# An attention and snake-MLP kernel: alpha loaded as 16 rows and transposed on TensorE, and the first w_in load cut to 256 columns

## The chip, the cores and the metric

The kernel runs on one core of a Trainium2 chip. The metric is the device time of one execution in microseconds, given as the median of several runs; beside it there is one execution taken by the hardware profiler. Engines are named as in the profile: PE is TensorE (PEld its weight loads), DVE is VectorE, ACT is ScalarE, POOL is GpSimd, SP is SyncE. A "q" behind an engine's name is its sequencer or its queue.

## The reference

Two stages. The first is chunked attention: 4 batches, 8 heads, 768 positions, head size 64. Each chunk of 32 queries sees 8 memory keys and up to 56 context keys (16 to the left, 32 of its own, 8 to the right).

```python
for c in range(nc):                       # 24 chunks of 32
    k_full = concat([mem_k, k[:, :, l_start:r_end]], axis=2)
    v_full = concat([mem_v, v[:, :, l_start:r_end]], axis=2)
    a = softmax(q_c @ k_full.T / sqrt(64))
    out[:, :, c_start:c_end] = a @ v_full
```

The second stage takes its output as x, with 3072 tokens of 512 numbers, and computes an MLP with 2048 inner columns:

```python
h = x @ w_in                              # 512 -> 2048
s = sin(alpha * h)                        # alpha: 2048 numbers, one per inner column
g = h + s * s / (alpha + 1e-09)
return g @ w_out                          # 2048 -> 512
```

## The kernel before, in words

Work is split by batch. For each batch of 768 tokens there is an attention part that fills `xT` (the transposed x) and an MLP part: 16 steps `ft` of 128 inner columns each (`l1`: 8 matmuls of 128x384 at line 400, a sine on ACT, a square on ACT, DVE or POOL, and a fused multiply-add on DVE into `gT`), and then the second matrix product (`l2`), whose pieces are mixed into the next batch's work by a `Stream`.

Batch 0 has nothing to overlap with but its own loads, and its attention part is written out by hand. `ORDER` is a string of pieces; `first_burst` walks through it, and every engine gets its instructions in that order. The pieces are: `k n` and `q n` transpose a pair of heads of k or q on PE (line 246, after some dummy matmuls on zeros at line 162, `spin`), and copy them out (k on DVE at lines 251 and 257, q on ACT, but `q 1` on DVE, line 264). `memk` transposes the memory keys on PE (line 363), copies them on DVE (line 367) and spreads them into `kTi` (line 149). `memv` converts the memory values and spreads them into `vw` (DVE, lines 142 and 143). `s n` are scores (PE, line 271), `e n` exponentials (ACT, line 287), `v n` the product with v (PE at line 302, DVE at 306 and 307), `x n` the transpose into `xT` (PE at line 323, a copy at line 326), `z n` dummy matmuls. The order starts:

```python
"k 0,q 0,memk 0,memv 0,k 1,s 0,e 0,z 1,s 1,e 1,q 1,k 2,s 2,e 2,s 3,v 0,q 2,..."
```

Loads go through two queues. SP's holds, in this order, mem_k in four parts (line 179), mem_v (line 180), and alpha (line 195), and later the stores of the output. POOL's holds the loads that change the type from float32 to bfloat16, in the order of the program: k pair 0, q pair 0, k 1, q 1 (line 107), the first quarter of v in four parts (line 139), k 2, q 2, k 3, q 3, the other three quarters of v in twelve parts, w_in in four parts (line 203), k and q of batch 1 (line 120), and w_out in two parts (line 209). [...] There are eight semaphores for these loads in turn, so each of them waits until the load eight places ahead of it has landed.

alpha is wanted as `alpha_sb`, 128 partitions by 16 columns, so that each `ft` has its 128 numbers down the partitions. The load before reads the vector of 2048 numbers in that transposed order: each element of four bytes goes to its own place. `inv_alpha` is computed from it on DVE (line 496) after the first burst, and the sines read `alpha_sb` as their scale (lines 409 and 412).

In PSUM there are two pools: `big` with three buffers of two banks, and `smp` with two buffers of one bank (tag `sm`), which the dummy matmuls, the q transposes, `memk` and others take in turn.

Of the kernel before, what the change touches and what calls it, by code (L numbers as in the profile page):

```python
# [9 lines left out]
P = 128  # L10
# [7 lines left out]
BF = mybir.dt.bfloat16  # L18
F32 = mybir.dt.float32
# [30 lines left out]
def kernel(  # L50
# [12 lines left out]
    nc = tc.nc  # L63
# [5 lines left out]
    HP = H // 2  # L69
    FT = d_ff // P  # L70
# [4 lines left out]
    consts = ctx.enter_context(tc.tile_pool(name="consts", bufs=1))  # L75
# [6 lines left out]
    smp = ctx.enter_context(tc.tile_pool(name="smp", bufs=2, space=bass.MemoryType.PSUM))  # L82
# [4 lines left out]
    ident = consts.tile([P, P], BF, name="ident")  # L87
# [8 lines left out]
    memkT = consts.tile([P, HP, 32], BF, name="memkT")  # L96
# [2 lines left out]
    memv_f = consts.tile([P, B, H, D], F32, name="memv_f")  # L99
    w_in_sb = consts.tile([P, KT, d_ff], BF, name="w_in_sb")  # L100
    w_out_sb = consts.tile([P, FT, d_model], BF, name="w_out_sb")
    alpha_sb = consts.tile([P, FT], F32, name="alpha_sb")
    inv_alpha = consts.tile([P, FT], F32, name="inv_alpha")

    def load_qk_pair(b, hp, kb, qb):
        for src, dst in ((k, kb), (q, qb)):
            nc.gpsimd.dma_start(
                dst[:, 2 * hp:2 * hp + 2].rearrange("p h r d -> p h (r d)"),
                src[b, 2 * hp:2 * hp + 2].rearrange("h (p r) d -> p h (r d)", p=P),
            )  # L110
# [15 lines left out]
    def load_v(b, n0, n1):  # L126


        vw = vws[b % 2].rearrange("p h j c -> p (h j) c")
        vf = v[b].rearrange("h s d -> (h s) d")  # L130
        vf = vf.rearrange("(n p) d -> p n d", p=QW)
        parts = (
            (vw[16:64, n0:n1, 0:D], vf[0:48, n0:n1]),
            (vw[72:120, n0:n1, 0:D], vf[48:96, n0:n1]),
            (vw[0:16, n0 + 1:n1, 0:D], vf[80:96, n0:n1 - 1]),
            (vw[120:128, n0:n1 - 1, 0:D], vf[0:8, n0 + 1:n1]),
        )
        for dst, src in parts:
            nc.gpsimd.dma_start(dst, src)  # L139

    def put_memv(b):
        (nc.vector.tensor_copy if b == 0 else nc.scalar.copy)(memv_st[64:72, b], memv_f[64:72, b])
        nc.vector.tensor_copy(
            vws[b % 2][64:72, :, :, 0:D],
            memv_st[64:72, b].unsqueeze(2).to_broadcast([NM, H, NJ, D]),
        )

    def put_memk(b):
        nc.vector.tensor_copy(
            kTi[:, :, 24:KW].rearrange("p g (j c) -> p g j c", c=104)[:, :, :, 40:40 + NM],  # L150
            memkT[:, :, NM * b:NM * b + NM].unsqueeze(2).to_broadcast([P, HP, NJ, NM]),
        )
# [4 lines left out]
    def spin(n, z=None):  # L157

        if z is None:
            z = smp.tile([P, 512], F32, name="z", tag="sm")  # L160
        for _ in range(n):
            nc.tensor.matmul(z[:], zeros[:, 0:P], zeros[:])  # L162
# [12 lines left out]
    load_v(0, 0, 16)  # L175
    for hp in range(2, HP):
        load_qk_pair(0, hp, *kq)
    for b in range(B):
        nc.sync.dma_start(memk_f[NM * b:NM * b + NM], mem_k[b].rearrange("h n d -> n h d"))
    nc.sync.dma_start(memv_f[64:72].rearrange("n b h d -> n (b h) d"),  # L180
                      mem_v.rearrange("b h n d -> n (b h) d"))
    for c, (a, e) in enumerate(((0, 16), (16, 56), (64, 120), (120, P), (32, 96), (64, 72))):
# [4 lines left out]
    nc.vector.tensor_add(rows[:, 3:4], rows[:, 2:3], rows[:, 3:4])  # L187
    nc.vector.tensor_scalar(
        out=biasm[:], in0=rows[:, 0:5], scalar1=1.0, scalar2=-NEG, op0=ALU.subtract, op1=ALU.mult)
    nc.scalar.copy(memk_bf[:], memk_f[:])  # L190
    load_v(0, 16, 32)
    load_v(0, 32, 48)
    load_v(0, 48, 64)
    with nc.allow_non_contiguous_dma(reason="alpha transpose load"):
        nc.sync.dma_start(alpha_sb[:], moe_alpha.rearrange("(ft p) -> p ft", p=P))

    nc.vector.memset(kTi[:, :, 0:16], 0.0)
    nc.vector.memset(kTi[:, :, 848:856], 0.0)
# [3 lines left out]
    def load_w_in(c0, c1):  # L202
        nc.gpsimd.dma_start(
            w_in_sb[:, :, c0:c1],
            moe_w_in[:, c0:c1].rearrange("(kt p) f -> p kt f", p=P),
        )
# [42 lines left out]
    def t_k(kb, hp):  # L249
        t = turn(kb, hp, hp < 2)  # L250
        nc.vector.tensor_copy(
            kTi[:, hp, 72:72 + 7 * 104].rearrange("p (s c) -> p s c", c=104)[:, :, 0:96]
            .rearrange("p s (a r) -> p s a r", r=6),
            t[:, :, 8:120].rearrange("p r (s a) -> p s a r", a=16),
        )
        for t0, c0 in ((0, 16), (120, 800)):
            nc.vector.tensor_copy(
                kTi[:, hp, c0:c0 + 48].rearrange("p (a r) -> p a r", r=6),
                t[:, :, t0:t0 + 8].rearrange("p r a -> p a r"),
            )  # L260

    def t_q(qb, hp, copy=nc.scalar.copy):
        t = turn(qb, hp)
        copy(qT[:, hp, :].rearrange("p (a r) -> p a r", r=6), t[:, :, :].rearrange("p r a -> p a r"))

    def qk(cells):

        sc = big.tile([P, 2, 512], F32, name="sc", tag="big")
        for c, (hp, j) in enumerate(cells):
            for e in range(2):  # L270
                nc.tensor.matmul(  # L271
                    sc[:, e, QW * c:QW * c + QW],
                    kTi[64 * e:64 * e + 64, hp, 104 * j:104 * j + P],
                    qT[64 * e:64 * e + 64, hp, QW * j:QW * j + QW],
                )
        return sc

    def exps(cells, sc):
        pt = pts[state["n"] % NPT]
        state["n"] += 1  # L280
        for m in range(3):
            cols = [((1 if j == 0 else 0), 4, (2 if j == NJ - 1 else 3))[m] for _, j in cells]
            c0 = 0
            for c1 in range(1, 5):
                if c1 < 4 and cols[c1] == cols[c0]:
                    continue
                nc.scalar.activation(  # L287
                    pt[:, 0:H * QW].rearrange("p (g e c) -> p e g c", g=4, e=2)[:, :, c0:c1, 32 * m:32 * m + 32],
                    sc[:, :, 0:4 * QW].rearrange("p g (e c) -> p g e c", e=4)[:, :, c0:c1, 32 * m:32 * m + 32],
                    ACTF.Exp, bias=biasm[:, cols[c0]:cols[c0] + 1], scale=0.125,  # L290
                )
                c0 = c1
        return pt
# [20 lines left out]
    def xt(dst, x_blk, ot, copy=nc.vector.tensor_copy, warm=0):  # L314
        if ot is None:
            z = smp.tile([P, 512], F32, name="z", tag="sm")
            spin(warm, z)
            xtp = z[:].bitcast(BF)[:, 0:KT * QW]
        else:
            xtp = ot[:].bitcast(BF)[:, 0, 640:640 + KT * QW]  # L320
        xtp = xtp.rearrange("p (k c) -> p k c", k=KT)
        for kt in range(KT):
            nc.tensor.transpose(  # L323
                xtp[:, kt, :], x_blk[:, 2 * kt:2 * kt + 2, :].rearrange("p e d -> p (e d)"), ident[0:QW, 0:QW]
            )
        copy(dst, xtp)
# [22 lines left out]
    def first_burst(kq):  # L349

        xT = xp.tile([P, KT, S], BF, name="xT")
        cells = [[(u // 2, 4 * (u % 2) + c) for c in range(4)] for u in range(8)]
        scl, ptl, xbl = {}, {}, {}
        for what, n in [t.split() for t in ORDER.split(",")]:
            n = int(n)
            if what == "k":
                t_k(kq[0], n)
            elif what == "q":
                t_q(kq[1], n, nc.vector.tensor_copy if n == 1 else nc.scalar.copy)
            elif what == "memk":  # L360
                mt = smp.tile([P, HP, 32], BF, name="mt", tag="sm")
                for hp in range(HP):
                    nc.tensor.transpose(
                        mt[:, hp, :],
                        memk_bf[0:32, 2 * hp:2 * hp + 2, :].rearrange("p e d -> p (e d)"),
                        ident[0:32, 0:32])
                nc.vector.tensor_copy(memkT[:], mt[:])
                put_memk(0)
            elif what == "memv":
                put_memv(0)  # L370
            elif what == "s":
                scl[n] = qk(cells[n])
            elif what == "e":
                ptl[n] = exps(cells[n], scl.pop(n))
            elif what == "z":
                spin(n)
            elif what == "v":
                x_blk, ot = pv(0, cells[n], ptl.pop(n))
                xbl[n] = x_blk, (ot if n < 2 else None)
            elif what == "x":  # L380
                hf = n % 2
                xt(xT[:, n // 2, HALF * hf:HALF * hf + HALF].rearrange("p (k c) -> p k c", k=KT),
                   *xbl.pop(n), nc.scalar.copy if n in (3, 4, 5, 6) else nc.vector.tensor_copy,
                   (0, 0, 2, 2, 1, 1, 0, 0)[n])
        return xT
# [100 lines left out]
            yield True  # L486


    for c0, c1 in ((0, 512), (512, 1024), (1024, 1536), (1536, 2048)):
        load_w_in(c0, c1)  # L490
    kq_next = load_qk(1)
    for c in range(2):
# [97 lines left out]
```

## Time and profile before

| | before |
|---|---|
| median of 5 runs | 232.31 us (232.03 to 233.26) |
| profiled execution, its own time | 232.98 us |
| its span | 231.2 us, 4560 instructions |
| PE busy | 217.0 us (94%) |
| DVE busy | 159.8 us (69%) |
| ACT busy | 152.7 us (66%) |
| POOL busy | 71.7 us (31%) |
| transfers of the software queue (POOL's) | 45600 packets, 14.41 MB |
| transfers of the hardware queue (SP's) | 6216 packets, 6.43 MB |
| alpha's load | 8 KB, issued at 2.55 us, landed 8.1 us later |
| first w_in load | 512 KB, issued at 19.89 us, landed 5.9 us later |

The span runs from the first to the last instruction of the profile; the execution's own time is 1.8 us longer. Times in the views are microseconds from the span's start. A view of groups or a timeline gives start, busy time, engine, line, operation, what is written and read, and in brackets the idle time of the engine before it and what ended it. The chain of waits is followed back from the last instruction to whatever released each step. The granted TensorE clock was 1.00 throughout.

### The profile page before, as it was taken

Reading aid. Unit: us, or ns where it says so; the run is one execution under the profiler, and the core shown is the slowest. Engines: PE = TensorE matmul, PEld = TensorE weight load, DVE = VectorE, ACT = ScalarE, POOL = GpSimd, SP = SyncE. Lnnn points to the kernel's source line nnn. Section 1 sums busy time; section 2 is a strip of 40 time slices with the busy share of each in tenths; the row PEclk is TensorE's granted clock in tenths of the full one; section 3 lists DMA queues with packets and bytes.
Section 4 is the critical chain, followed back from the end, with each engine's and each line's share of the span. In section 5 each row is a group of like instructions: output and inputs, shape, how many; then the busy total and the mean of one; then the engine's idle time right before and its main releaser. Section 6 shows DMA issues by size and latency. Waiting matters only on the chain.

```text
span 231.2 us, 4560 instructions
## 1 busy us (share of the span) xinstructions
PE 217.0 (94%) x1807; PEld 122.2 (53%) x1836; DVE 159.8 (69%) x287; ACT 152.7 (66%) x246; POOL 71.7 (31%) x84
## 2 busy tenths in 40 slices
PE   7987899899989999999999999998999999899994
PEld 2455555546456556554555656664555555453453
DVE  5667688988568897987566789887565458784110
ACT  2579789792987387888664877978665676880110
POOL 8899523576812115167200314020000020100000
PEclk9999999999999999999999999999999999999999
DMA  5999999999999900119992101010111010101112
GB/s 81 147 177 97 200 206 205 207 193 117 130 240 176 124 23 0 45 11 194 162 154 68 45 0 48 0 45 3 45 48 72 19 50 0 45 0 48 73 64 91
DMA packets 51837, 21.13 MB, mean 91 GB/s; under 512 B 36328, under 2 KB 48872, under 8 KB 51816
## 3 DMA queue, kind: packets, MB, share of 16 engines
q0 software_dynamic: 45600, 14.41, 76.0%
q1 hardware_dynamic: 6216, 6.43, 9.0%
q8 instruction: 14, 0.23, 0.5%
q14 instruction: 7, 0.06, 0.1%
HBM read 28.93 MB, written 6.29 MB: 152 GB/s over the span
## 4 chain that ended last, share of the span: by engine, by line
PE 64%; DVE 12%; ACT 10%; issue 6%; POOL 3%; DMA 2%; POOLq 1%; DVEq 0%; ACTq 0%
PE o L479 27%; PE hT L400 21%; DVE gT L429 5%; PE ot L302 3%; ACT u L412 3%; ACT pt L287 3%; PE sc L271 3%; DVE s L421 3%; DMA k_bf<-in_k_dram 2%; DVE x_blk L307 2%; PE o L449 2%; PE tt_a L243 2%; PE ot L323 2%; PE o L468 2%; POOL s L417 1%
## 5 line engine op out<-in xcount | busy, mean ns | idle before, releaser
L400 PE MATMUL hT<-xT,w_in_sb 128*128 128x384 bf16 x488 | 87.1, 326 | 2.9 <-DVE gT L429 2.8
L479 PE MATMUL o<-w_out_sb,gT 128*128 128x512 bf16 x313 | 85.0, 380 | 1.7 <-issue 0.5
L429 DVE SCALAR_TENSOR_TENSOR gT<-s,inv_alpha,hT 128x768 bf16<-128x768 f32 x61 | 61.1, 1012 | 19.9 <-ACT s L415 11.1
L412 ACT ACTIVATE u<-hT,alpha_sb 128x768 f32<-128x768 f32 x61 | 54.7, 897 | 23.8 <-PE hT L400 22.8
L400 PEld LDWEIGHTS <-w_in_sb 128*128 128x128 bf16 x512 | 49.2, 97 | 37.6 <-issue 3.8
L287 ACT ACTIVATE pt<-sc,biasm 128x256 bf16<-128x256 f32 (+2 forms) x104 | 39.1, 470 | 14.5 <-PE sc L271 14.4
L479 PEld LDWEIGHTS <-gT 128*128 128x128 bf16 x336 | 29.2, 97 | 24.3 <-DVE gT L429 1.2
L417 POOL TENSOR_TENSOR s<-u 128x768 f32<-128x768 f32 x9 | 13.2, 1465 | 83.8 <-ACT u L412 61.3
L415 ACT ACTIVATE s<-u 128x768 f32<-128x768 f32 x32 | 27.0, 844 | 1.0
L421 DVE TENSOR_TENSOR s<-u 128x768 f32<-128x768 f32 x23 | 24.3, 1055 | 2.3 <-ACT u L412 2.2
L139 POOL DMA_DIRECT2D vw<-in_v_dram x28 | 24.1, 871 | 0.5 <-DMA vw<-in_v_dram 0.2
L307 DVE TENSOR_TENSOR x_blk<-ot,rinv 96x512 bf16<-96x512 f32 x32 | 22.0, 686 | 1.1
L217 POOL COPY pr<-q_bf 128x768 bf16<-128x768 bf16 x12 | 10.7, 895 | 33.9 <-PE tt_a L243 22.2
L437 DVE COPY o_sb<-o 128x512 f32<-128x512 f32 x12 | 8.3, 688 | 15.6 <-PE o L479 15.5
L437 ACT COPY o_sb<-o 128x512 f32<-128x512 f32 x11 | 6.4, 582 | 17.9 <-PE o L479 17.9
L306 DVE RECIPROCAL rinv<-ot 96x8 f32<-96x8 f32 x32 | 6.4, 201 | 15.5 <-PE ot L302 15.3
L302 PEld LDWEIGHTS <-pt 128*128 128x128 bf16 x256 | 11.7, 97 | 6.4 <-issue 2.0
L302 PE MATMUL ot<-vw,pt 128*128 128x65 bf16 x256 | 13.0, 193 | 1.1 <-ACT pt L287 0.9
L243 PEld LDWEIGHTS <-pr 128*128 128x128 bf16 x144 | 10.0, 98 | 6.2 <-DVE pr L217 1.2
L271 PEld LDWEIGHTS <-kTi 64*128 64x128 bf16 x256 | 6.8, 94 | 11.4 <-PE ot L323 5.5
L323 PEld LDWEIGHTS <-x_blk 96*128 96x128 bf16 x128 | 8.4, 97 | 7.9 <-DVE x_blk L307 2.8
L162 PE MATMUL z<-zeros 128*128 128x512 bf16 x30 | 10.9, 465 | 1.4 <-DVE zeros L155 1.2
(74 smaller groups left out, 169.7 us busy)
## 6 DMA issues: line engine op xcount, KB each, us to landing
out_dram<-o_sb SPq DMA_DIRECT2D x23, 256.0 KB, 2.5
k_bf<-in_k_dram POOLq DMA_DIRECT2D x3, 768.0 KB, 10.9
q_bf<-in_q_dram POOLq DMA_DIRECT2D x3, 768.0 KB, 15.0
vw<-in_v_dram POOLq DMA_DIRECT2D x6, 384.0 KB, 15.1
w_in_sb<-in_moe_w_in_dram POOLq DMA_DIRECT2D x4, 512.0 KB, 8.6
w_out_sb<-in_moe_w_out_dram POOLq DMA_DIRECT2D x2, 1024.0 KB, 24.2
k_bf<-in_k_dram POOLq DMA_DIRECT2D x4, 192.0 KB, 5.5
q_bf<-in_q_dram POOLq DMA_DIRECT2D x4, 192.0 KB, 5.7
```

The source lines that it names most:

```text
L139: nc.gpsimd.dma_start(dst, src)
L287: nc.scalar.activation(pt[:, 0:H * QW].rearrange("p (g e c) -> p e g c", g=4, e=2)[:, :, c0:c1, 32 * m:32 * m + 32], sc[:, :, 0:4 * QW].re ...
L302: nc.tensor.matmul(otv[:, n // 4, n % 4, :], pt[:, QW * n:QW * n + P], vws[b % 2][:, 2 * hp + n % 2, j, 0:D + 1])
L307: nc.vector.tensor_tensor(out=x_blk[:].rearrange("p (g e) d -> p g e d", g=2), in0=otv[0:QW, :, :, 0:D], in1=rv.unsqueeze(3).to_broadcast( ...
L400: nc.tensor.matmul(hts[hf][:, 0:HALF], w_in_sb[:, kt, P * ft:P * ft + P], xT[:, kt, HALF * hf:HALF * hf + HALF], start=(kt == 0), stop=(kt ...
L412: nc.scalar.activation(u[:], hT[:, :, 0:HALF], ACTF.Sin, scale=alpha_sb[:, ft:ft + 1])
L415: nc.scalar.activation(s2[:], u[:], ACTF.Square)
L417: nc.gpsimd.tensor_tensor(out=s2[:], in0=u[:], in1=u[:], op=ALU.mult)
L421: nc.vector.tensor_tensor(out=s2[:], in0=u[:], in1=u[:], op=ALU.mult)
L429: nc.vector.scalar_tensor_tensor(out=gv, in0=s2[:], scalar=inv_alpha[:, ft:ft + 1], in1=hT[:, :, 0:HALF], op0=ALU.mult, op1=ALU.add)
L437: (nc.vector.tensor_copy if s % 2 == 0 else nc.scalar.copy)(o_sb[:], o[:])
L479: nc.tensor.matmul(o[:], gT[:, ft, P * s:P * s + P], w_out_sb[:, ft, :], start=(ft == 0), stop=(ft == FT - 1),)
```

## The change

alpha is now loaded as it lies in memory: 16 rows of 128 numbers, 512 bytes each, into `alpha_r` on 16 partitions. The load stands first in SP's queue, ahead of mem_k and mem_v. In the piece `memk`, PE transposes it with a float32 identity of 16x16 into columns 256 to 271 of the same PSUM tile that takes the memory keys' transposes, and DVE copies it out to `alpha_sb` after the memory keys are spread. The small identity is a DVE copy of a corner of the bfloat16 one. The PSUM tile of `memk` is now a whole bank of float32, of which the first part is used as bfloat16.

Second, the four loads of w_in have other bounds: 256, 512, 512 and 768 columns in place of four times 512.

```diff
+    alpha_r = consts.tile([FT, P], F32, name="alpha_r")
+    ident_f = consts.tile([FT, FT], F32, name="ident_f")
     alpha_sb = consts.tile([P, FT], F32, name="alpha_sb")
...
         load_qk_pair(0, hp, *kq)
+    nc.sync.dma_start(alpha_r[:], moe_alpha.rearrange("(ft p) -> ft p", p=P))
     for b in range(B):
         nc.sync.dma_start(memk_f[NM * b:NM * b + NM], mem_k[b].rearrange("h n d -> n h d"))
...
+    nc.vector.tensor_copy(ident_f[:], ident[0:FT, 0:FT])
     nc.scalar.copy(memk_bf[:], memk_f[:])
...
-    with nc.allow_non_contiguous_dma(reason="alpha transpose load"):
-        nc.sync.dma_start(alpha_sb[:], moe_alpha.rearrange("(ft p) -> p ft", p=P))
...
             elif what == "memk":
-                mt = smp.tile([P, HP, 32], BF, name="mt", tag="sm")
+                z = smp.tile([P, 512], F32, name="z", tag="sm")
+                mt = z[:].bitcast(BF)[:, 0:HP * 32].rearrange("p (g c) -> p g c", g=HP)
+                nc.tensor.transpose(z[:, 256:256 + FT], alpha_r[:], ident_f[:])
                 for hp in range(HP):
                     nc.tensor.transpose(
                         mt[:, hp, :],
                         memk_bf[0:32, 2 * hp:2 * hp + 2, :].rearrange("p e d -> p (e d)"),
                         ident[0:32, 0:32])
-                nc.vector.tensor_copy(memkT[:], mt[:])
+                nc.vector.tensor_copy(memkT[:], mt)
                 put_memk(0)
+                nc.vector.tensor_copy(alpha_sb[:], z[:, 256:256 + FT])
...
-    for c0, c1 in ((0, 512), (512, 1024), (1024, 1536), (1536, 2048)):
+    for c0, c1 in ((0, 256), (256, 768), (768, 1280), (1280, 2048)):
         load_w_in(c0, c1)
```

## The prediction

> **What bounds the kernel now.** I read the page first. PE is 94% busy over the span, so a few tenths of a microsecond at the start matter only if they delay PE's real work. The row of DMA tenths stands at 9 through the first third, so the transfers are a candidate there, and the chain of waits tells where they end last. In it (microseconds of start, length, what):
>
> ```profile
> 4.90 2.63 POOL vw L139 x4
> 7.53 5.67 DMA k_bf<-in_k_dram
> 13.20 0.04 issue
> 13.24 0.53 PE z L246 x12
> 13.77 0.45 PE sc L271 x16
> ```
>
> One transfer, the third k pair, stands on the chain; its 5.67 us are all of the 2% that the page's chain gives to transfers. From 13.24 on everything is engine work. So what the change can win by transfers, it wins before 13.24.
>
> Next, what the transfer engines did while that k pair was waiting (window 5 to 7 us, share of 16 engines):
>
> ```profile
> DMA packets 2108, 0.22 MB, mean 112 GB/s; under 512 B 1862, under 2 KB 2108, under 8 KB 2108
> q0 software_dynamic: 264, 0.19, 70.7%
> q1 hardware_dynamic: 1844, 0.03, 60.8%
> ```
>
> 1844 packets of the hardware queue, nearly all alpha's 2048 elements, carry 0.03 MB and take 60.8% of 2 us. The stretches by time show the hole (last number: GB/s):
>
> ```profile
> 6.00:7.00 1.00, 1.00 (x15) 0.37 (x13) 0.00 (x0) 0.53 (x1) 1.00 (x3) 1.00 1.32 73
> 7.00:8.00 1.00, 1.00 (x16) 0.37 (x13) 0.79 (x2) 0.00 (x0) 1.00 (x2) 1.00 1.26 160
> ```
>
> Last, the timeline round 13.24, engine by engine; brackets give idle time before and its releaser:
>
> ```profile
> 9.58 1.30 DVE L143 COPY vw<-memv_st 8x4096 bf16<-8x4096 bf16 x1
> 10.89 0.86 DVE L251 COPY kTi<-zb 128x672 bf16<-128x672 bf16 x1
> 11.91 0.96 DVE L264 COPY qT<-z 128x768 bf16<-128x768 bf16 x1
> ...
> 10.71 0.71 POOL L107 DMA_DIRECT2D q_bf<-in_q_dram  x1 [0.85 <-DMA q_bf<-in_q_dram]
> ...
> 13.24 0.53 PE L246 MATMUL z<-ident,k_bf 128*64 128x128 bf16 x12 [0.62 <-DMA k_bf<-in_k_dram]
> ...
> 14.08 1.35 ACT L287 ACTIVATE pt<-sc,biasm 128x64 bf16<-128x64 f32 x4 [1.39 <-PE sc L271]
> ```
>
> PE waited 0.62 us for the k pair. But DVE runs without a gap from 8.61 to 12.87, and its last piece, the second q pair (11.91 + 0.96 = 12.87), is what the scores at 13.70 need as well. So behind the transfer, DVE is 0.8 us away from being the limit (13.70 against 12.87 + 0.05).
>
> **The change, part by part.**
>
> *Removed: 2048 packets.* Hardware-queue time after 5 us: 60.8% of 2 us = 1.22, then 10.2% of 2 us = 0.20 (7 to 9 us) and 1.6% of 2 us = 0.03: 1.45 us of all 16 engines. By bytes: 5 to 7 us moved 223 KB where its neighbours move about 170 a microsecond, so 117 KB short, 0.7 us. The k pair therefore lands 0.7 to 1.45 us earlier, at 11.8 to 12.5. PE is free for it at 12.62 (its dummy matmuls of line 162 run to 11.80 + 0.82). So the whole wait of 0.62 goes, and no more than that.
>
> *POOL moves up.* Each load waits until the one eight places ahead has landed: 0.85 us before the last q pair, 0.24 before the next v load (11.66), 0.20 at 16.59. They sum to 1.29 and go wholly or mostly, so the w_in loads are issued 1.0 to 1.3 us earlier than 19.89, the k, q and w_out loads behind them too.
>
> *First w_in load of 256 columns.* It landed at 19.89 + 5.9 = 25.8; its first weight load ran at 26.35, straight after the last transposes, so nothing waited: 0.55 us of slack. The second load landed 1.7 us after the first (20.68 + 6.8), so half the columns save about 0.85, and with POOL's advance the first part lands near 23.9. Columns 256 to 767, about 25.7, are first used at ft 2, 26.39 + 2 x 1.3 = 29.0. Worth nothing by itself; if the load were late, it would cost what exceeds the slack.
>
> *SP's order.* alpha's issue (0.41 us in the trace) now stands ahead of mem_k and mem_v. mem_k lands at about 5.0 in place of 4.61, its cast on ACT (with the table load ahead of it) ends near 6.95 in place of 6.53, and PE takes it at 8.31. mem_v is used at 9.13. Hidden: 1.4 us of cover.
>
> *The identity's copy on DVE.* Between a 0.07 memset and the 0.23 copies, in front of an idle stretch of 2.06 us (before 7.21). Hidden.
>
> *The float32 transpose on PE.* No float32 matmul is in the trace. Nearest below: the memk transposes, four in 0.26 us, 0.05 apart. Above: a 128x512 matmul at 0.43 at the start. I take 0.15, near the small rows. It stands ahead of the memk transposes (8.31), for which DVE already waited 0.31, so it delays both PE and DVE by its whole length. Behind it on PE: memk, the second k pair, the first scores.
>
> *The alpha copy on DVE.* Step between two small copies of line 257 0.11; reciprocal of 128x16 0.24. I take 0.2; it lies in DVE's gapless stretch, ahead of mem_v, the second k pair's copy and the q copy.
>
> *What POOL's advance does to DVE.* The mem_v spread of line 143 (SBUF to SBUF) ran at 9.58 mostly in POOL's 0.85 us pause. It comes four times:
>
> ```profile
> L143 DVE COPY vw<-memv_st x4: 1218/1258/2075, 9.6 to 127.2; 8x4096 bf16<-8x4096 bf16 x4
> ```
>
> The slow one, 2.08 at 59.44, lies wholly within POOL's v loads (57.78 to 62.7); 1.22 is with POOL idle. With the pause gone, this copy runs beside POOL's issues from end to end: 0 to 0.78 more (2.08 less 1.30). In the trace 0.45 us of overlap with the same kind of issue (9.58 to 9.86, 10.71 to 10.88) cost 0.08, which over the whole copy makes 0.23, so 0.15 more than now; rounded up I take 0.2, since the issues beside it are again mostly k and q pairs.
>
> [...]
>
> **Sum.** DVE's delay: 0.15 + 0.2 + 0.2 = 0.55. The q copy ends at 13.42, so scores can start at 13.48. PE's own path: 12.62 + 0.15, and 0.46 from the transposes to the scores as now: 13.23. The later one counts: 13.48 against 13.70, a gain of about 0.2. ACT idled 1.39 before these exponentials, and then works to 24.5 with one wait of 0.27, so the 0.2 goes through to the first w_in matmul; after that no transfer stands on the chain, and PE's work is the same, so it stays to the end. The profiled execution took 232.98 (span 231.2, 1.8 around it); less 0.2 is 232.8. The median of the runs is 0.67 below it: 232.1.
>
> Ends: least delay 0.05 + 0.1 + 0 = 0.15, then PE's 13.13 counts, gain 0.57. Most: 0.43 + 0.25 + 0.78 = 1.46, scores at 14.38, loss 0.68. The forecast's own range is 231.7 to 233.0.
>
> **Rivals.**
>
> *Faster.* The transfers hold more than the chain shows: some of the waits called "issue" before PE's weight loads (0.42 and 0.63 us, line 246) are late data too, and with these gone ACT's idle 1.39 and its 0.27 close: up to 1.66, 230.65, at least the 1.2 that makes it faster here. For it: transfer engines at 9 tenths throughout. Against: DVE's gapless 8.61 to 12.87, which no transfer shortens.
>
> *Slower.* The spread of line 143 loses POOL's pause and is held behind a k, a q and a v issue in a row. Price: the k and q issues (0.72 + 0.71) bring it 0.8 late, the v issue 0.75 more: 1.55. With 0.35 to 0.65 for the other two, DVE is 1.9 to 2.2 late, scores at 14.8 to 15.1, loss 1.1 to 1.4: up to 233.7. It decides from a DVE delay of 0.78 for any loss, 1.9 for one over 0.5%. Against: 2.08 was the worst under continuous issue.
>
> *It does not do what it says.* Loads issued after alpha's packets were gone took as long (the last k pair 6.2, the last q pair 5.6, against 5.7), so the k pair may land hardly earlier. Then the delay of 0.55 hides in the 0.78: 232.3, no change.
>
> **Numbers.** Forecast 0.44; no effect 0.16; faster rival 0.24; slower rival 0.16. Within 0.5% (1.16 us, about what a measurement of this kernel can tell from no change) are the first two: 0.60. The range 230.8 to 233.4 leaves out the far parts of both outer rivals, about 0.2.
>
> **What would show it.** Right: PE's wait for the k pair at line 246 gone, second q copy on DVE ending near 13.4, scores near 13.5, w_in issued near 18.8, first w_in matmul near 26.2. Wrong: the spread over 2 us long or starting after 10.4, a float32 transpose over 0.4, a k pair that lands at 13 still, or any wait for w_in.

## The result, and the profile after

| | before | after |
|---|---|---|
| median beside each other | 234.41 us (231.92 to 238.14, 80 runs) | 233.0 us (231.52 to 235.11, 43 runs) |
| ratio after / before | | 1.0004, 95% interval 0.9989 to 1.002 |
| profiled execution, its span | 232.98, 231.2 us | 233.6, 231.8 us |
| packets of the hardware queue | 6216 | 4184 |

The verdict is "same". The ratio leaves out executions over 1.5% above the fastest of their kernel, which explains how it can be 1.0004 while the medians are 1.4 us apart. So there are two results. By the ratio the change is worth nothing. But 38 of the 80 executions of the kernel before were above 235.2 us, and none of the kernel after. The experiments had to explain both.

First the steps that the prediction counted. The transfer engines between 5 and 7 us, in the kernel after:

```profile
DMA packets 615, 0.36 MB, mean 181 GB/s; under 512 B 199, under 2 KB 615, under 8 KB 615
q0 software_dynamic: 440, 0.32, 112.8%
q1 hardware_dynamic: 175, 0.04, 12.8%
```

The hardware queue has 175 packets in place of 1844 and takes 12.8% in place of 60.8%, and the bytes moved rise from 0.22 to 0.36 MB. The timeline of the kernel after (start, length, engine, line; brackets: idle before and its releaser):

```profile
8.68 0.23 PE L365 MATMUL z<-ident_f,alpha_r 16*128 16x16 f32 x1
...
9.05 0.23 DVE L371 COPY memkT<-z 128x128 bf16<-128x128 bf16 x1 [0.38 <-PE z L367]
...
9.45 0.34 DVE L373 COPY alpha_sb<-z 128x16 f32<-128x16 f32 x1
...
10.30 1.22 DVE L145 COPY vw<-memv_st 8x4096 bf16<-8x4096 bf16 x1
...
12.53 0.94 DVE L266 COPY qT<-z 128x768 bf16<-128x768 bf16 x1
...
13.53 0.37 PEld L273 LDWEIGHTS <-kTi 64*128 64x128 bf16 x16 [0.18 <-DVE qT L266]
13.53 0.52 PE L273 MATMUL sc<-qT,kTi 64*128 64x96 bf16 x16
...
13.92 0.99 ACT L289 ACTIVATE pt<-sc,biasm 128x64 bf16<-128x64 f32 x3 [0.78 <-PE sc L273]
```

The k pair is no longer the releaser. The scores now wait for DVE's q copy, which ends at 12.53 + 0.94 = 13.47; before they started at 13.70, now at 13.53. That is the limit that was predicted, and the exponentials are 0.16 earlier (13.92 against 14.08). But the chain of waits shows that the transfers are not gone from it:

```profile
9.69 7.51 DMA q_bf<-in_q_dram
17.20 0.04 issue
17.24 0.55 PE z L248 x12
```

The last q pair took 7.51 us and landed at 17.20. The trace records sixteen completions for each of POOL's loads (96 for the six loads of a semaphore), and the profile gives times as shares of 16 transfer engines; I take one completion for one engine's share, which the trace doesn't say. Fifteen shares of this load had landed by 15.66, the last at 17.20. POOL's timeline shows what hangs on it:

```profile
10.41 5.37 POOL L141 DMA_DIRECT2D vw<-in_v_dram  x7
17.48 3.23 POOL L141 DMA_DIRECT2D vw<-in_v_dram  x5 [1.70 <-DMA q_bf<-in_q_dram]
20.71 1.55 POOL L205 DMA_DIRECT2D w_in_sb<-in_moe_w_in_dram  x2
```

A load eight places behind waited 1.70 us for that one share, and w_in was issued at 20.71, not earlier than before (19.89) but 0.82 later. The first w_in matmul started at 26.53 (before 26.39). A last loss comes at batch 1:

```profile
64.51 0.40 PE L304 MATMUL ot<-vw,pt 128*128 128x65 bf16 x8 [0.96 <-ACT pt L289]
```

The same matmuls ran at 63.58 before, without a wait:

```profile
63.58 0.41 PE L302 MATMUL ot<-vw,pt 128*128 128x65 bf16 x8
```

The releaser named is ACT, but the last share of batch 1's v load landed at 64.37 (before at 62.72), 0.14 us ahead of this start, so I read the wait as v's. The profiles of e1 and e3 below support it: there v is the releaser named, and the start is 0.13 and 0.14 behind the last share. PE's matmul just ahead of this wait began at 63.16, before at 63.36: so until then the kernel after was 0.2 ahead. At the end it is late by 0.6, which is the difference of the two spans.

### The profile page after: what moved, and what is told of

The parts are those of the page before. It is cut to its first block, busy times and chain, and to the rows that moved or that the text cites. A ratio compares the mean times of both kernels' runs of the same rounds, so it can differ in the third digit from the quotient of the medians.

```text
span 231.8 us, 4564 instructions
## 1 busy us (share of the span) xinstructions
PE 217.5 (94%) x1808; PEld 122.4 (53%) x1837; DVE 159.8 (69%) x289; ACT 152.9 (66%) x246; POOL 72.5 (31%) x84
## 3 DMA queue, kind: packets, MB, share of 16 engines
q1 hardware_dynamic: 4184, 6.43, 8.5%
## 4 chain that ended last, share of the span: by engine, by line
PE 63%; DVE 11%; ACT 11%; issue 6%; POOL 4%; DMA 3%; POOLq 1%; DVEq 0%; ACTq 0%
PE o L484 27%; PE hT L405 21%; DVE gT L434 5%; ACT u L417 4%; DMA q_bf<-in_q_dram 3%; PE ot L304 3%; PE sc L273 3%; DVE x_blk L309 2%; ACT pt L289 2%; DVE s L426 2%; ACT s L420 2%; PE tt_a L245 2%; PE ot L325 2%; PE o L473 2%; PE o L454 1%
## 5 line engine op out<-in xcount | busy, mean ns | idle before, releaser
L141 POOL DMA_DIRECT2D vw<-in_v_dram x28 | 24.7, 894 | 2.6 <-DMA q_bf<-in_q_dram 1.7
```

## The experiments

The kernel before ran again beside each group of experiments. Line numbers are those of each kernel. The granted clock of every execution is recorded too, and it becomes the main reading below.

### Which half does what

**e1: the kernel after, once more**, to see what of its profile repeats.

> The changed kernel once more. Theory A: in its first profile the last q pair landed at 17.20 us because one 16 KB instruction fetch at 14.59 us fell on one of the 16 transfer engines that still had 1/16 of that pair to move; where such a fetch falls varies from execution to execution, so here the pair's last share lands more than 1 us after the others only by chance, POOL's pause of 1.70 us before the v load may be gone, and the time is within 0.2% of the kernel before. Rival B: the lateness is systematic, made by POOL's earlier issues (more loads in flight), so the last q pair lands at 17 us again, POOL pauses 1.5 us or more again, w_in is issued at 20.5 or later, and the ratio is 1.000 to 1.003.

Measured: median 232.87 us (232.44 to 234.25, 12 runs), ratio 0.9991 (0.9953 to 1.003). In its profile the first exponentials were 0.89 us ahead of before, not 0.16, POOL waited 0.92 for the last q pair, w_in was issued at 19.78, PE waited 0.50 for the second w_in load, and the end was 0.3 ahead. So neither the early gain nor the losses behind it have a fixed size: one profile of a kernel is one draw.

**e2: alpha's part alone**, w_in in four times 512 columns.

```diff
-    for c0, c1 in ((0, 256), (256, 768), (768, 1280), (1280, 2048)):
+    for c0, c1 in ((0, 512), (512, 1024), (1024, 1536), (1536, 2048)):
```

> Only the alpha part of the change; w_in in four loads of 512 columns as before. Theory (both A and B): the w_in cut is worth nothing, since no matmul waited for w_in; the time equals that of the whole change within 0.1%, and the first w_in weight load starts right behind the last transposes. Rival C: the smaller first load matters once POOL issues w_in late (20.7 us in the changed kernel); then the first w_in matmul waits here, up to 0.9 us, and the ratio is 1.002 to 1.004.

Measured: median 235.04 us (232.34 to 237.82), ratio 1.001 (0.995 to 1.007). The profiled execution (235.51, span 233.7) was 0.86 ahead until 25 us. Then, in its timeline of PE:

```profile
25.36 0.34 PE L325 MATMUL z<-ident,x_blk 96*128 96x96 bf16 x4 [0.49 <-DVE x_blk L309]
27.51 5.75 PE L405 MATMUL hT<-xT,w_in_sb 128*128 128x384 bf16 x24 [1.81 <-DMA w_in_sb<-in_moe_w_in_dram]
```

PE waits 1.81 us for the first w_in load, whose fifteenth share landed at 24.93 and whose last at 27.46. And the 24 matmuls behind it take 5.75 us, where before they took 4.07:

```profile
26.39 4.07 PE L400 MATMUL hT<-xT,w_in_sb 128*128 128x384 bf16 x24
```

Its stretches by time show why; the column behind the engines' busy times, third from the end, is the granted clock of PE:

```profile
26.00:27.50 1.50, 0.00 (x0) 0.00 (x0) 0.34 (x3) 0.69 (x1) 0.04 (x1) 1.00 1.24 204
27.50:27.90 0.40, 0.39 (x3) 0.27 (x4) 0.00 (x0) 0.00 (x0) 0.00 (x0) 0.98 1.23 205
27.90:31.30 3.40, 3.40 (x12) 1.57 (x11) 0.41 (x1) 0.90 (x1) 0.00 (x0) 0.50 1.24 207
31.30:33.00 1.70, 1.70 (x12) 1.04 (x11) 1.57 (x2) 0.97 (x2) 0.00 (x0) 1.00 1.27 202
```

From 27.9 to 31.3 PE runs at half its clock. Half of 3.4 us is 1.7, so the late share costs 1.8 for the wait and 1.7 for the clock: from 0.86 ahead to 2.8 behind at the end of these 24 matmuls (33.26 against 30.46).

**e3: the new cuts of w_in alone**, in the kernel before.

```diff
-    for c0, c1 in ((0, 512), (512, 1024), (1024, 1536), (1536, 2048)):
+    for c0, c1 in ((0, 256), (256, 768), (768, 1280), (1280, 2048)):
```

> Only the w_in bounds of 256, 512, 512 and 768 columns; alpha loaded element by element as before. Theory: no wait for w_in in the kernel before, so the ratio is 1.000 within 0.001 and the first w_in matmul starts near 26.4 us. Rival C: below 0.998.

Measured: median 232.63 us (232.15 to 234.47), ratio 0.998 (0.9942 to 1.0018). Alpha's packets stay, and yet the executions near 237 are gone. Its profiled execution was a long one for another reason (PE waited 1.46 us for batch 1's v load at 65.39). With alpha's packets in place, PE also waited 0.85 us for the first q pair and 1.13 for the third k pair.

**e4: no load of alpha**, alpha_sb filled with ones, so the sines are of other numbers; and **e6: the same with the new cuts**.

```diff
-        nc.sync.dma_start(alpha_sb[:], moe_alpha.rearrange("(ft p) -> p ft", p=P))
+    nc.vector.memset(alpha_sb[:], 1.0)
```

> The kernel before without any load of alpha: alpha_sb is filled with ones by DVE before its other memsets, so the sine's scale and the reciprocal are not the reference's. No transpose, no copy, no packets. If the packets were worth what the prediction said, the third k pair lands at 11.8 to 12.5 us, scores at 13.70 us in the profile before start near 13.1, and the ratio is 0.997 to 0.998. If the delay of the last loads is systematic (B), the early gain is there but the last q pair still lands near 17 us and the ratio is about 1.000. If the packets cost nothing, the k pair lands near 13.2 us again.

> No load of alpha (alpha_sb filled with ones, as in the earlier run) together with the new w_in bounds. The most that the alpha part can bring, without its transpose and copies. Theory A: no wait for the first w_in part, ratio 0.996 to 0.998, no execution above 235. Rival (the alpha part is worth nothing): 0.999 to 1.001, like the w_in bounds alone (0.998, interval 0.994 to 1.002).

Measured: e4 234.0 us (231.51 to 236.05), ratio 0.9998 (0.9949 to 1.0048); e6 232.76 (231.82 to 234.3), ratio 0.9976 (0.9936 to 1.0016). e4 bounds what alpha's load can be worth, since it has neither packets nor transpose: in its profile 0.44 early at 14 us and 0.7 at the end, in the median nothing that can be told apart. In e6's profile the last share of a k pair was late, and PE waited 1.7 us for it. Here too it is the cut that goes with the missing long executions.

**e8: the alpha transpose and copy moved**, out of DVE's tight stretch to behind the fifth exponentials.

```diff
-    ... "s 5,e 5,z 1,v 2,..."
+    ... "s 5,e 5,al 0,z 1,v 2,..."
```

> The changed kernel with alpha's transpose and its copy moved out of the memk piece to a piece of its own after the exponentials of step 5, where DVE has idle time; nothing else. By the prediction's sum the two cost DVE 0.35 us on the path to the scores of step 2, so these start 0.3 us earlier against the second q pair's copy than in the changed kernel (DVE's stretch from the memk copy to the end of that q copy is 0.3 us shorter), and the ratio against the changed kernel is 0.998 to 0.999. If the early stretch is not what counts (theory A), the stretch shortens but the ratio is the changed kernel's, 0.999 to 1.000, within its interval.

Measured: 233.0 us (231.99 to 234.28), ratio 0.9979 (0.994 to 1.0019). The first exponentials were where the kernel after has them (13.91 against 13.92). But DVE's stretch from the memory keys' copy to the end of the q copy, forecast to be 0.3 shorter, was 0.2 longer (8.82 to 13.47 against 9.05 to 13.47): the two steps on the memory values took 0.65 and 1.48 us in place of 0.42 and 1.22. So the profile doesn't show what the transpose and copy cost; in the median nothing can be told apart.

### Is a late first w_in load what counts?

**e5: the first w_in part issued ahead of the last quarter of v**, in the kernel after.

```diff
     load_v(0, 32, 48)
+    load_w_in(0, 256)
     load_v(0, 48, 64)
```

> The changed kernel with the first w_in part (256 columns) moved in POOL's queue ahead of the last quarter of v (four small loads, 2.6 us of POOL's time). Theory A: the early gain of the alpha part (0.9 us at 13 to 14 us in two profiles) is lost because single late shares of loads hit the first two w_in parts and, through the full transfer queue, batch 1's v load at 64 us; the engines were half idle at 18 to 22 us, so an earlier large load uses them, the first w_in part lands before 23 us, no matmul waits for w_in, batch 1's v load lands up to 1 us earlier, and the ratio is 0.995 to 0.998. Rival: the queue is full later anyway and the last v quarter now lands too late for head pair 3 (its first use at 23.9 us in the kernel before), PE waits there up to 1 us, ratio 1.000 to 1.004.

Measured: 233.84 us (232.79 to 235.08), ratio 1.0035 (0.9994 to 1.0076). The first w_in part landed at 21.03, well in time, but the last v quarter came late (its last share at 23.77), PE had gaps of 0.60, 0.39 and 0.49 us between 23.2 and 26.1, and then the same picture without any wait for w_in:

```profile
26.30 5.75 PE L406 MATMUL hT<-xT,w_in_sb 128*128 128x384 bf16 x24
```

```profile
26.00:27.00 1.00, 0.89 (x7) 0.53 (x8) 0.56 (x4) 0.98 (x2) 0.35 (x1) 0.77 1.24 205
27.00:28.00 1.00, 1.00 (x5) 0.47 (x4) 0.09 (x2) 0.44 (x1) 0.00 (x0) 0.50 1.24 205
28.00:29.90 1.90, 1.90 (x7) 0.89 (x6) 0.10 (x1) 0.90 (x1) 0.00 (x0) 0.50 1.17 205
29.90:31.00 1.10, 1.10 (x8) 0.71 (x7) 0.98 (x2) 0.22 (x1) 0.00 (x0) 0.98 1.18 214
```

The clock is half from about 26.5 to 29.9, again 3.4 us. Several short gaps did what one long gap did in e2. The last gap, of 0.49, is in the kernel before too.

**The recorded clocks of all executions** then sort themselves. Of the 136 executions of the kernel before that ran beside the experiments, 70 had a mean granted clock of 0.997 or more (median 232.85 us), 50 had 0.990 to 0.993 (median 235.90) and 16 had 0.984 or 0.985 (median 236.88). One stretch of 3.41 us at half clock in a span of 231 makes 1 - 0.5 x 3.41 / 231 = 0.993, two make 0.985. By kernel, the executions below 0.997:

| first w_in load | kernels |
|---|---|
| 512 columns | before 66 of 136, e2 7 of 12, e4 5 of 12 |
| 256 columns, in its place | after and e1 1 of 56, e3 1 of 12, e6 1 of 12, e8 0 of 12 |
| 256 columns, v late | e5 6 of 12 |

Three runs put this to the test: theory C says that PE idles for w_in and its clock falls behind that idle time.

**e13: the place of the wait filled with dummy matmuls**, in the kernel before.

```diff
-    ... "x 6,x 7"
+    ... "x 6,x 7,z 6"
```

> The kernel before, with 6 more dummy matmuls (z 6, some 1.3 us of PE) at the end of the order, between batch 0's last transposes and its first w_in matmul. Theory C (in about half of the executions of the kernel before PE idles for the first w_in load, and its clock falls behind that idle time): PE has work where it idled, the granted clock is 0.997 or more in at least 11 of 12 executions, and none is over 235; the price is up to 1.3 us less what PE idled there anyway: median 232.8 to 234.0. Rival (the lower clock comes from the chip, or from another place in the run): a third or more of the executions still at 0.993 or below, up to 238.

Measured: 234.31 us (233.6 to 235.18), ratio 1.0024 (0.9995 to 1.0053); clock 0.998 or more in 12 of 12, while 14 of the 31 executions of the kernel before beside it were at 0.993 or below. The median is above the forecast (232.8 to 234.0), and one execution is over 235. In its profile the share was late as in e2 (fifteenth 25.19, last 27.18), and PE had work:

```profile
25.52 1.46 PE L162 MATMUL z<-zeros 128*128 128x512 bf16 x6
27.23 4.07 PE L400 MATMUL hT<-xT,w_in_sb 128*128 128x384 bf16 x24 [0.25 <-DMA w_in_sb<-in_moe_w_in_dram]
```

The 24 matmuls take 4.07 us. The dummies cost their 1.3 us in every execution (234.31 against 232.99 for the full-clock executions of the kernel before beside it), so as a cure they are no better than the disease; as a test they say that the idle time of PE lowers the clock, not the late data as such.

**e14: the wait forced**, the first two w_in loads of the kernel before exchanged, and **e15: forced and filled**.

```diff
-    for c0, c1 in ((0, 512), (512, 1024), (1024, 1536), (1536, 2048)):
+    for c0, c1 in ((512, 1024), (0, 512), (1024, 1536), (1536, 2048)):
# e15 also:
-    ... "x 6,x 7"
+    ... "x 6,x 7,z 10"
```

> The kernel before, with its first two w_in loads exchanged: columns 0 to 511, which the first matmuls need, are loaded second and land near 28.3 us, where the second load landed, so PE waits some 2 us in every execution. Theory C: the granted clock is 0.985 to 0.993 in every execution, the timeline shows half the clock for about 3.5 us behind the wait, and the time is 2.0 for the wait plus about 1.7 for the clock: 235.5 to 237. Rival (the wait costs itself alone): clock 1.0, 234 to 234.8.

> e14 with 10 dummy matmuls of 512 columns (z 10, 2.1 us) at the end of the order, so that PE is busy while it waits. Theory C: the wait stays, the clock does not fall (0.997 or more): 234 to 235, 1.5 to 2 us under e14. Rival (the clock falls for another reason than PE's idle time): as e14.

Measured: e14 237.05 us (234.09 to 239.95), ratio 1.0067 (1.0011 to 1.0122); clock below 0.997 in 9 of 12, not in all. Its twelve fall in groups: three at full clock, 234.09 to 234.23; three at 0.991 to 0.993, 235.70 to 235.96; six at 0.986 or below, 238.14 to 239.95. From the first to the second it is 1.7 us by their medians (234.19, 235.86), the price of one half-clock stretch. The profiled one has two of them:

```profile
30.42 3.04 PE L400 MATMUL hT<-xT,w_in_sb 128*128 128x384 bf16 x9 [4.52 <-DMA w_in_sb<-in_moe_w_in_dram]
```

```profile
25.00:26.40 1.40, 0.41 (x6) 0.20 (x4) 0.96 (x4) 1.28 (x2) 1.40 (x2) 1.00 1.23 200
26.50:30.40 3.90, 0.00 (x0) 0.00 (x0) 0.18 (x1) 0.38 (x1) 0.12 (x1) 0.50 1.24 203
30.40:33.30 2.90, 2.88 (x10) 1.36 (x11) 0.00 (x0) 0.10 (x1) 0.00 (x0) 0.50 1.25 205
33.40:35.00 1.60, 1.60 (x12) 0.96 (x10) 0.87 (x1) 1.07 (x2) 0.00 (x0) 1.00 1.30 203
```

Half from 26.5 to 33.3, 6.8 us. e15: 235.5 us (234.34 to 239.38), ratio 1.0077 (1.0034 to 1.012), 1.55 under e14, with 9 of 12 at full clock; 12 of 12 and at most 235 were forecast. Where a share came late even for ten dummies, the clock fell all the same:

```profile
26.41 2.32 PE L162 MATMUL z<-zeros 128*128 128x512 bf16 x10
31.14 2.30 PE L400 MATMUL hT<-xT,w_in_sb 128*128 128x384 bf16 x9 [2.41 <-DMA w_in_sb<-in_moe_w_in_dram]
```

```profile
28.80:31.00 2.20, 0.00 (x0) 0.00 (x0) 0.00 (x0) 0.00 (x0) 0.00 (x0) 1.00 1.24 205
31.00:31.90 0.90, 0.77 (x5) 0.51 (x6) 0.00 (x0) 0.00 (x0) 0.00 (x0) 1.00 1.25 208
32.00:35.30 3.30, 3.30 (x12) 1.62 (x11) 1.09 (x2) 0.90 (x1) 0.00 (x0) 0.50 1.28 204
```

Here the clock is still full throughout the idle time and falls 0.8 us after the work has begun again; in e14 it fell at 26.5, 0.6 us after the last transpose. So the fall comes at set times of its own, not so long after the idle time began. The clock records of the traces show these times: in every profile the clock changes only at whole multiples of 3.41 us after the first record of full clock (in e2 full for 23.89 us, 7 of them, then half for one; in e14 full for 20.48, 6 of them, then half for two). So each profile can be cut into its own windows of 3.41 us, and PE's idle time can be read in each:

| profile | window, us | PE idle in it, us | clock in the next window |
|---|---|---|---|
| before | 23.43 to 26.84 | 0.75 | full |
| e13 | 25.34 to 28.75 | 0.25 | full |
| e2 | 24.47 to 27.89 | 2.35 | half |
| e5 | 23.12 to 26.53 | 1.48 | half |
| e14 | 23.06 to 26.48 | 1.50 | half |
| e14 | 26.48 to 29.89 | 3.41 | half |
| e15 | 25.13 to 28.54 | 0.74 | full |
| e15 | 28.54 to 31.96 | 2.41 | half |
| e6 | 10.73 to 14.14 | 1.69 | full |

In this table, windows with up to 0.75 us of idle time were followed by full clock, those with 2.35 and more by half. Between them, e6 (1.69, full) against e5 and e14 (1.48 and 1.50, half) says that idle time alone, roughly as the trace gives it, doesn't decide it. In e14 the first half stretch came from the window before the long wait, and the wait itself added the second.

The half-clock stretches were 3.4, 3.4, 6.8 and 3.4 us long (e2, e5, e14, e15). Windows that were idle for less than half their length were followed by one (1.48 in e5, 1.50 in e14), and gaps of PE well under 3.41 us stood ahead of one: 1.81 in e2, 2.41 in e15 and three of 0.4 to 0.6 in e5. The first full-clock record lies anywhere from 3.90 to 7.24 us in the profiles, so the same gap can fall within one window in one execution and across two in the next, which fits e14's three executions at full clock; their windows are not recorded.

### Why is one share late?

The last share came 2.0 to 2.5 us after the fifteenth in the profiles of e2, e13, e14 and e15, and 0.05 to 0.7 after it in those of before, e4, e7, e10 and e12, all with a first load of 512 columns. Theory A of the expectations is that an instruction fetch of PE (14 packets of 16 KB in a run, the queue called "instruction" in the profile's list) falls on one transfer engine just then; the second fetch came between 20.3 and 21.8 us in most profiles. That it is PE's is inferred: with 60 more instructions on PE it came at 18.51 and 18.23 (e7, e12 below), against 21.22 in the kernel before.

The shares of the loads in between show how the lateness builds up. In e2, e13, e14 and e15 the last share of the v parts that landed between 19.9 and 21.9 us is at most 0.1 behind, that of the last v parts, which landed behind the fetch (from 22.6 us), 1.2 to 1.5, and that of all four w_in loads 1.9 to 2.5: one lag is carried from load to load. That fits a fetch (0.9 to 1.2 us long there) as its beginning. But in e4 the fetch at 20.73 and a last v share 1.28 behind went with a w_in share only 0.08 behind, while in e14 the fetch at 20.78 went with 2.15: the fetch's time alone doesn't decide it.

**e7, e12: 40 dummies of 128 columns** at the start of the kernel before, in place of 10 of 512 (60 instructions more on PE, the fetch 3 us earlier, at 18.51 and 18.23); **e9: the same in the kernel after**. **e10, e11: 20 dummies of 256 columns** in before and after (fetch at 19.55 and 20.81).

```diff
-    spin(10)
+    z0 = smp.tile([P, 512], F32, name="z", tag="sm")
+    for _ in range(40):                    # e10, e11: 20, and 256 columns
+        nc.tensor.matmul(z0[:, 0:P], zeros[:, 0:P], zeros[:, 0:P])
```

> The kernel before with its first ten dummy matmuls of 512 columns replaced by forty of 128 columns: about the same PE time, 60 PE instructions more, so PE's 16 KB instruction fetches come about 60 instructions, near 2 us, earlier against the work. Theory A (a fetch on one transfer engine makes that engine's share of the next loads late): the fetch of 21.2 us moves to about 19 us, before the w_in load, its lag is worked off while the engines are half idle, the first w_in load's last share lands within 0.3 us of the others in the profile, and hardly any execution takes over 235 us (of the kernel before 14 of 35 did in the last job). Rival D (one engine is slower for another reason, or the w_in load is late with no fetch near): the spread stays as wide as before.

> e7 once more (the kernel before with 40 dummies of 128 columns), beside the others on one chip. Theory A: median 232.0 to 232.6, none over 234. If e7 was luck of its call: a median like that of the kernel before in this call, with executions over 235.

> The kernel after, with 40 dummy matmuls of 128 columns at the start in place of 10 of 512 (60 more instructions on PE, so that PE's second instruction fetch comes at about 18.5 us, as in e7, and not at 20.3 to 21.4). Theory A (the two kernels differ little between their undisturbed executions; what spreads them is a load of which one share lands late, a fetch being on the way): the early gain of 0.16 to 0.9 at the first exponentials of batch 0 is kept as far as w_in, all shares of the first w_in load land within 0.3 us of each other; median 231.9 to 232.5, spread under 2 us. Theory B (e7's gain comes from PE's earlier clock or finer dummies alone, the fetch is of no matter): the change's effect adds nothing or costs as before: 232.3 to 233.0, with some executions over 234.

> The kernel before, with 20 dummies of 256 columns in place of 10 of 512 (20 more instructions on PE, so that the second fetch comes near 20.3 us, where it was in e2). Theory A: the fetch falls beside the first w_in load, whose last share lands up to 2 us after the others in many executions: median 233.5 to 235.5, executions up to 238. Theory B (finer dummies are what helped in e7): a third of e7's gain or more: median at or under 233.0, hardly any execution over 235.

> The kernel after, with 20 dummies of 256 columns (second fetch near 20 us). Theory A: the first w_in load, of 256 columns, has room for a share that is 2 us late, so the worst executions of e10 are missing: median 232.5 to 233.5, none over 235.5. Rival (the cut protects from nothing, the spread belongs to the chip or to the moment): as e10, with the same share of executions over 235.5.

| | first w_in load | median, us | ratio to before | clock below 0.997 |
|---|---|---|---|---|
| e7 | 512 | 232.31 (231.84 to 233.11) | 0.9939 (0.9897 to 0.9981) | 0 of 12 |
| e12 | 512 | 232.71 (231.91 to 234.38) | 0.9958 (0.9916 to 0.9999) | 1 of 12 |
| e9 | 256 | 232.61 (232.04 to 234.16) | 0.9947 (0.9902 to 0.9991) | 0 of 12 |
| e10 | 512 | 234.12 (231.91 to 236.86) | 1.001 (0.9962 to 1.0058) | 3 of 12 |
| e11 | 256 | 232.42 (231.83 to 234.97) | 0.9975 (0.9929 to 1.0022) | 1 of 11 |

Three things follow. The 2 by 2 of e10, e11, e12 and e9 ran side by side on one chip: with the fetch near 20 us the small first load takes 1.7 us off the median (234.12 to 232.42), with the fetch at 18.4 it takes off 0.1 (232.71 to 232.61). That fits the cut and the dummies curing the same thing, one of them being enough, though these are eleven or twelve executions each, and the intervals of e10 and e11 overlap. Second, e9 and e12 missed their forecasts of at most 232.5 and 232.6 by 0.1 and reached 234.16 and 234.38, so some spread has another source. In e9's profile the last share of the first w_in load was 0.54 behind, where at most 0.3 was forecast, and that of the second 1.72: moving the fetch doesn't rid a kernel of late shares. Third, that it is the fetch stays a theory: moving it went with the missing late shares, but the small dummies change PE's start as well, e10 with its fetch at 19.55 had its load in time in the profiled execution, and the trace doesn't say which transfer engine carried which packet. No version beat the others by more than the runs can tell: e7 is the fastest by its median, and the kernel after with the same dummies (e9) is within 0.3 of it.

## Why the prediction was right or wrong

**Right in what sets the scores, by luck in the number: the k pair, the DVE stretch and its sum.** The forecast was that PE's wait of 0.62 goes and that DVE's q copy, ending at 13.42, then sets the scores at 13.48. They were set by it, at 13.47 and 13.53. The k pair landed at 12.75, 0.45 earlier than before (0.7 to 1.45 forecast), ahead of PE. But DVE's delay, 0.55 forecast and 0.60 measured, was made of other parts. 0.37 of it is in no term of the sum: PE came to the piece `memk` at 8.68, before at 8.31. The granted clock of 1.00 that is given for the whole profile hides why: the trace's first record of full clock stands at 6.37 us before and at 7.24 after. Ahead of it the dummies of 512 columns start 0.43 us apart, behind it 0.22, so PE ran slow for 0.87 us longer.

The other parts: the transpose, 0.15 in the sum, held the memory keys' transposes by 0.09 (8.68 to 8.77; its own 0.23 overlaps them). DVE's stretch from the memory keys' copy to the end of the q copy grew by 0.16 (8.61 to 12.87 before, 9.05 to 13.47 after), where 0.4 was forecast: the alpha copy and the spread of the memory keys under it added 0.28, and the spread of line 143, for which 0.2 was added, took 0.08 less (1.22 against 1.30). That these come out within 0.05 of the sum is luck.

The spread took 1.22 to 1.30 us in most profiles and 1.48 in e1, e7, e8 and e11, so the 0.2 was of the right order there. In the profile after, POOL's issue beside it took 1.45 us instead of 0.75: the second rival had the right conflict and, here, the wrong loser. DVE's copy had started 0.11 us earlier (10.30 against 10.41) and took 1.22; POOL was slowed, by 0.7 us and not by the 1.11 that were left of the copy. In e1 both were slowed (copy 1.48, issue 1.24). What decides which of them is slowed, and by how much, these runs don't show.

**Wrong in size: alpha ahead in SP's queue.** mem_k was to land 0.4 later, at 5.0. It landed at 5.97 in the profile after and at 5.6 to 6.0 wherever alpha stands first, against 3.6 to 4.6 elsewhere. In the profile after this stayed hidden; in e1, where PE was early, PE waited 0.20 us for its cast.

**Wrong in size, sometimes: the early gain.** 0.2 was forecast for it, 0.16 measured in the profile after, but 0.89 in e1 and 0.86 in e2, the same early part. There PE came out of its slow start sooner (full clock from 4.59 and 3.99; four dummy matmuls at 3.73 us took 1.46 us in e1, 1.91 before), and with alpha's packets gone the first q pair no longer held it (landed at 6.84 in e1, at 7.73 before). e3 is the counterpart: full clock from 4.52, but with the packets, and PE waited 0.85 for that q pair. The prediction took DVE's gapless stretch from one profile as fixed; its start moves with PE.

**Wrong: "after that no transfer stands on the chain ... so it stays to the end".** The last q pair (7.51 us on the chain after) and batch 1's v load gave the 0.16 back and left the profile after 0.6 behind. In e1 0.3 of 0.89 was left. Over the executions at full clock nothing of it is left: median 232.93 of 55 of the kernel after and e1, 232.85 of 70 of the kernel before.

**Wrong: "the w_in loads are issued 1.0 to 1.3 us earlier".** POOL's three pauses were summed as if each wait ended with the mean load. They end with the last share of one load, and one late share gave a pause of 1.70 where 1.29 in all was to go: w_in 0.82 later in the profile after, 0.11 earlier in e1.

**Wrong, and the largest: "worth nothing by itself".** The slack of 0.55 us in front of the first w_in matmul was read from one execution in which all shares came in step (the last 0.05 behind the fifteenth). The half load's gain was misread too: the second load landed at 28.38, not at 27.48, 2.55 us behind the first, so half the columns save more than the 0.85 of the sum. In about half of the executions of the kernel before (66 of 136) PE's clock is lowered, which costs 3.0 us and more of the median (235.90 and 236.88 against 232.85). e2's profile, e13 and e14 show how: a late share, PE idle in front of its densest work, and 1.7 us for each half-clock stretch on top of the wait. With the cut it is 1 of 56, and e3 and e2 show that it is the cut: 1 of 12 with it alone, 7 of 12 without it. "If the load were late, it would cost what exceeds the slack" also missed the second price, the clock. That every one of the 66 had a late w_in share is inferred; e2 is the profiled one.

**The number.** 232.1 was forecast and 233.0 measured. Of these 0.9 us, 0.54 is the base: the five runs it was taken from had a median of 232.31, the 70 executions at full clock 232.85. Another 0.2 is the gain that didn't last; 0.15 stays unassigned. The change of the median against the kernel before beside it, 1.4 us, came from a step priced at zero.

## What to carry to other kernels

Ask of every load that PE waits for not whether it was in time in the profile, but how much later its last share may come: here 2 to 2.5 us, so a slack of 0.55 was none. A gap of PE just ahead of dense matmuls had two prices here, the wait (1.81 us in e2) and a stretch at half clock (1.7 us), and the second shows as steps in the mean granted clock of each execution (0.993, 0.985), which is to be read for all runs before the profile of one is believed. Here a small first piece of the load cured this at no cost that the runs show (e3: ratio 0.998), unless another load came late in its place (e5); dummies in the gap kept the clock up too, in 12 of 12 executions of e13 and 9 of 12 of e15, but are paid in every execution (1.3 us in e13).

## What the runs showed of the hardware

- PE's granted clock fell to half for 3.4 us (6.8 in e14) after idle time of 1.81 us (e2), 2.41 (e15) and three gaps of 0.4 to 0.6 (e5). The records change only in steps of 3.41 us from the first full-clock record; a window of 3.41 us with 1.48 us or more of idle time was followed by half clock in e2, e5, e14 and e15, one with 1.69 in e6 was not.
- The first record of full clock came at 3.90 (e6) to 7.24 us (after); dummies of 512 columns started 0.43 us apart ahead of it, 0.22 behind it.
- The last of a load's sixteen completions came 2.0 to 2.5 us after the fifteenth (first w_in load in e2, e13, e14, e15), and the lag stayed at 1.9 to 2.5 through the four w_in loads; the cause is open.
- A float32 transpose of 16x128 took 0.23 us on PE, of which the next transpose waited 0.09; a copy of 128x16 float32 from PSUM took 0.34 us on DVE (0.17 in e1).
- Beside POOL's issues a DVE copy of 8x4096 took 1.22 to 1.30 us, or 1.48 (e1, e7, e8, e11); a POOL issue beside it took 1.45 in the profile after and 1.24 in e1 in place of 0.75.
